# Transposing all of Q by DMA in a fused attention, spectral and feed-forward kernel

## The chip, the cores and the metric

The kernel runs on one core of a Trainium2 chip. The metric is the device time of one execution in microseconds (us), lower is better. Before the change the median of three runs was 299.42 us (298.74 to 299.74). One core has five engines that work side by side, each through its own instruction stream in a fixed order: TensorE (PE; PEld is its weight load), VectorE (DVE), ScalarE (ACT), GpSimd (POOL) and SyncE (SP). Transfers go through sixteen DMA engines. In this kernel GpSimd issues nearly all loads ("software_dynamic" in the profile), and SyncE issues five small ones at the start, the DMA transposes, the stores and some small copies ("hardware_dynamic").

## The reference

Attention with sorted keys and values (4 batches, 8 heads, sequence 768, head width 64), then a two-dimensional Fourier transform over sequence and model width (512), then layer normalisation and a feed-forward part. Cut to what matters:

```python
for _ in range(5):                       # Sinkhorn: P becomes a soft permutation of 8 blocks
    P = P - np.max(P, axis=-1, keepdims=True)
    P = np.exp(P)
    P = P / (np.sum(P, axis=-1, keepdims=True) + 1e-09)
    P = P / (np.sum(P, axis=-2, keepdims=True) + 1e-09)
k_sorted = np.einsum('bhij,bhjcd->bhicd', P, k_b).reshape(B, H, S, D)
v_sorted = np.einsum('bhij,bhjcd->bhicd', P, v_b).reshape(B, H, S, D)
# per block of 96 rows: softmax(q k^T / 8) v
...
X = np.fft.fft(np.fft.fft(x, axis=1), axis=2)
u = x + np.real(X)
un = (u - mu) / np.sqrt(var + 1e-06)
return u + np.maximum(un @ w_ch1, 0.0) @ w_ch2
```

The scores need Q with the head width on the partitions, so Q has to be transposed. So do the normalised rows `un` ahead of the feed-forward matmuls.

## The kernel before

The kernel does not run its statements in the order in which they are written. Each operation is handed to a planner, with what it reads and writes, a priority, and for each engine that may do it a pair of times: how long it holds the engine and when its result is there. The planner simulates the engines once, at build time, and the order that comes out is frozen into the instruction streams. A wrong pair of times gives no wrong result, but an order that fits another machine.

Q of batches 2 and 3 is loaded in small pieces and transposed by DMA. Q of batches 0 and 1 is loaded in long pieces, copied into another order of columns, transposed on TensorE and moved from its bank to SBUF:

```python
QB = (2, 3)
...
many("qr", 2, [128, 6, 128], F16)
many("qt", 3, [128, S], F16)
...
def load_qk(nm, b, hf, prio):
    src = {"k": k, "q": q}[nm]
    if nm == "q" and b in QB:
        for h in range(4):                                  # pieces of 64 elements
            load(kq[:, slot[nm, b, hf], :].rearrange(
                "p (a r h d) -> p a h r d", a=2, h=2, d=D)[:, h // 2, h % 2],
                src[b, 4 * hf + h].rearrange("(r p) d -> p r d", r=6),
                196608, [("kq", slot[nm, b, hf])], prio + 0.01 * h)
        return
    load(kq[:, slot[nm, b, hf], :].rearrange("p (h x) -> p h x", h=4),
         src[b, 4 * hf:4 * hf + 4, :, :].rearrange(
             "h (p r) d -> p h (r d)", r=6), 786432,
         [("kq", slot[nm, b, hf])], prio)
...
def q_copy(b, hp):                                          # batches 0 and 1 only
    if b in QB:
        return
    qr = Buf("qr")
    ...
    P.add(c, lambda e: copy(e, qr.ap.rearrange("p r (h d) -> p r h d", h=2), src), ...)
...
    if b in QB:                                             # in kqt(b, hp)
        qt = Buf("qt")
        P.add({"SP": (1.4, 3.4)}, lambda _: nc.sync.dma_start_transpose(
            qt.ap.rearrange("p (r s) -> p r s", r=6),
            kq[:, slot["q", b, hf], 768 * hl:768 * hl + 768]),
            r=[("kq", slot["q", b, hf])], w=[qt], tag="qX")
        return
    ...
    for r in range(6):
        nc.tensor.matmul(p16[:, 128 * r:128 * r + 128], qr.ap[:, r],
                         idh, is_transpose=True)
    ...
    P.add(c, lambda e: copy(e, qt.ap.rearrange("p (s r) -> p s r", r=6),
          pt.ap.bitcast(F16)[:, 0:768].rearrange("p (r s) -> p s r", r=6)),
          r=[pt], w=[qt], tag="qtev")
```

Note the pair `(1.4, 3.4)`: the planner counts on a transpose landing 3.4 us after SyncE took it up.

The normalised rows of batches 1 to 3 go by DMA as well (`if b > 0:` ahead of `dma_start_transpose(ut..., un)`), those of batch 0 on TensorE. When the planner chooses the next operation of an engine, one of higher priority that lacks a free buffer holds back those of lower priority on the same engine that want a buffer of the same pool.

The softmax here doesn't subtract the row's maximum and nothing guards it: scores larger than these inputs give would overflow.

## Time and profile before

| what | before |
|---|---|
| median of 3 runs | 299.42 us |
| span of the profiled run | 299.0 us |
| first matmul of V's mixing | 30.5 us |
| VectorE busy, 45 to 60 us | 14.84 of 15 us |
| first feed-forward matmul | 76.0 us |
| from there to the end | 223.0 us |
| a transpose of Q (128 x 768) from issue to landing, 98 to 107 us (two of four are recorded) | 2.7 us |

How to read it: the kernel has a stage up to 76 us in which attention and the Fourier part of the first batch are prepared with all engines at work, and a stage after it in which TensorE is full. What moves the border between them moves the end. One caution on this profile: the profiled run took 300.78 us, and later runs of the same kernel lay between 294.3 and 301.9 us (39 in one call, median 297.32). On one core a run counts as slow if it lies over 1.5% above the fastest, so this profiled run and some of the timed ones count as slow; with one core there is no second die to compare with.

### The profile page before, as it was taken

How to read it: one execution, taken by the hardware profiler on the slowest of the kernel's cores; microseconds unless marked ns; L12 is line 12 of the kernel's file. 1: busy time of each engine (PE TensorE's matmuls, PEld its weight loads, DVE VectorE, ACT ScalarE, POOL GpSimd, SP SyncE). 2: the span in 40 equal slices, each digit the busy share in tenths (PEclk: the TensorE clock that was granted, in tenths of full speed). 3: DMA queues.
4: the chain of work that ended last, by engine and by line, in shares of the span. 5: the costliest groups of instructions: out<-in, count | busy, mean ns of one | idle time of the engine just before them, and what ended most of it. 6: DMA issues, size and time to landing. Idle time of an engine off the chain costs nothing.

```text
span 299.0 us, 5829 instructions
## 1 busy us (share of the span) xinstructions
PE 271.8 (91%) x2332; PEld 166.4 (56%) x2332; DVE 178.3 (60%) x395; ACT 153.3 (51%) x307; POOL 55.1 (18%) x91
## 2 busy tenths in 40 slices
PE   0499988884999999899999999999999999999994
PEld 0266976763556656555556645545645645645641
DVE  4797589999699999786249954314605315312001
ACT  2575579862647797468237703613721631641710
POOL 8964212012800036030002000200200010010000
PEclk9999999996699999999999999999999999999999
DMA  7999999980920249825010210031021121121002
GB/s 116 218 286 216 216 206 213 203 111 15 67 17 2 58 98 162 150 13 107 35 71 15 55 70 35 20 105 38 15 53 70 37 53 70 37 54 70 37 0 105
DMA packets 43025, 26.32 MB, mean 88 GB/s; under 512 B 29834, under 2 KB 38552, under 8 KB 42996
## 3 DMA queue, kind: packets, MB, share of 16 engines
q0 software_dynamic: 22576, 15.16, 33.3%
q1 hardware_dynamic: 20422, 10.78, 12.4%
q8 instruction: 18, 0.29, 0.4%
q14 instruction: 9, 0.07, 0.1%
HBM read 28.95 MB, written 6.29 MB: 118 GB/s over the span
## 4 chain that ended last, share of the span: by engine, by line
PE 72%; DVE 16%; DMA 4%; ACT 2%; issue 2%; POOL 2%; DVEq 0%; ACTq 0%; POOLq 0%
PE bank L1112 28%; PE bank L1091 25%; PE bank L635 3%; DVE rt L905 2%; DMA kq<-in_q_dram 2%; PE bank L1005 2%; PE bank L952 2%; PE bank L851 2%; PE bank L891 2%; DMA out_dram<-u 2%; PE bank L638 2%; DVE pmt L919 2%; PE bank L797 2%; DVE u L1020 1%; PE bank L1012 1%
## 5 line engine op out<-in xcount | busy, mean ns | idle before, releaser
L1103 ACT ACTIVATE hr<-bank 128x384 f16<-128x384 f32 x111 | 54.1, 490 | 79.9 <-PE bank L1091 79.7
L1091 PE MATMUL bank<-ut,w1sb 128*128 128x384 f16 x512 | 93.4, 331 | 0.7 <-DVE hr L1100 0.7
L1112 PE MATMUL bank<-w2sb,hr 128*128 128x512 f16 x384 | 89.0, 379 | 0.0
L1091 PEld LDWEIGHTS <-w1sb 128*128 128x128 f16 x512 | 49.5, 99 | 36.1 <-issue 3.0
L1112 PEld LDWEIGHTS <-hr 128*128 128x128 f16 x384 | 36.5, 98 | 40.6 <-issue 0.2
L1120 DVE TENSOR_TENSOR u<-bank,u 128x512 f32<-128x512 f32 x24 | 16.6, 690 | 51.5 <-PE bank L1112 51.0
L1020 DVE SCALAR_TENSOR_TENSOR u<-rt,bank 128x512 f32<-128x512 f16 x24 | 16.1, 678 | 35.6 <-PE bank L1012 29.7
L860 ACT ACTIVATE ex<-bank 96x384 f32<-96x384 f32 x64 | 27.9, 485 | 8.3 <-PE bank L851 6.5
L1033 POOL TENSOR_SCALAR mv<-mv 128x3 f32<-128x3 f32 x8 | 2.6, 320 | 141.8 <-DVE mv L1028 139.6
L1052 ACT ACTIVATE un<-u,nm,ny 128x512 f16<-128x512 f32 x14 | 11.4, 811 | 14.6 <-POOL nm L1042 9.0
L395 POOL DMA_DIRECT2D kq<-in_q_dram x20 | 17.7, 905 | 4.2 <-ACT qr L571 1.9
L891 PE MATMUL bank<-vsf,eb 97*128 97x65 f16 x384 | 15.8, 195 | 2.7 <-DVE u L1020 1.3
L905 DVE TENSOR_TENSOR rt<-bank,rz 128x384 f16<-128x384 f32 x32 | 17.3, 550 | 0.4
L874 ACT ACTIVATE eb<-ex,negone 96x384 f16<-96x384 f32 x29 | 17.5, 614 | 0.2
L891 PEld LDWEIGHTS <-eb 97*128 97x128 f16 x384 | 14.3, 98 | 4.8 <-issue 2.9
L571 ACT CAST vsf<-bank 96x512 f16<-96x512 f32 x19 | 13.9, 790 | 4.3 <-PE bank L638 3.4
L1026 DVE BATCH_NORM_STATS2 st<-u 128x6 f32<-128x512 f32 x24 | 15.9, 682 | 0.2
L395 POOL DMA_DIRECT2D kq<-in_k_dram x8 | 6.5, 808 | 49.9 <-issue 27.8
L826 PE MATMUL bank<-pack,qr 128*128 128x128 f16 x48 | 5.3, 264 | 11.0 <-ACT qr L571 10.2
L635 PE MATMUL bank<-bdv,vcx 128*128 128x128 f16 (+1 forms) x128 | 14.2, 238 | 1.1 <-ACT bdv L571 1.1
L872 DVE TENSOR_SCALAR eb<-ex 96x384 f16<-96x384 f32 x35 | 13.1, 377 | 1.7 <-ACT ex L860 1.6
L797 PE MATMUL bank<-bdk,kq 128*64 128x128 f16 x192 | 11.8, 247 | 1.5 <-DVE u L1020 1.0
(114 smaller groups left out, 337.8 us busy)
## 6 DMA issues: line engine op xcount, KB each, us to landing
out_dram<-u SPq DMA_DIRECT2D x24, 256.0 KB, 2.0
kq<-in_k_dram POOLq DMA_DIRECT2D x8, 384.0 KB, 9.2
w1sb<-in_moe_w_ch_dram POOLq DMA_DIRECT2D x4, 512.0 KB, 15.2
w2sb<-in_moe_w_ch_dram POOLq DMA_DIRECT2D x4, 512.0 KB, 19.0
kq<-in_q_dram POOLq DMA_DIRECT2D x4, 384.0 KB, 11.3
hr<-in_v_dram POOLq DMA_DIRECT2D x2, 768.0 KB, 11.5
kq<-in_v_dram POOLq DMA_DIRECT2D x2, 768.0 KB, 21.3
kq<-in_q_dram POOLq DMA_DIRECT2D x16, 96.0 KB, 6.0
```

The source lines that it names most:

```text
L395: return P.add({eng: c}, lambda _: e.dma_start(dst, src), r=r, w=w, prio=prio, nbytes=nbytes, tag="load", after=after)
L635: nc.tensor.matmul(o, vcx[:, 96 * d:96 * d + m], bd, start=True, stop=(t == 1))
L797: nc.tensor.matmul(ps.ap[64 * h2:64 * h2 + 64, 128 * r3:128 * r3 + 128], k16[:, 2 * hl + h2, 3 * half + r3, :], bdk[:, 2 * hp + h2].rearra ...
L860: nc.scalar.activation(ex.ap, pss[h2].ap[0:96, 0:384], AF.Exp, scale=SCALE),
L874: nc.scalar.activation(ed, src, AF.Identity, bias=negone[0:96])
L891: nc.tensor.matmul(po.ap[:, 65 * T:65 * T + 65], eb.ap[:, e0:e0 + 128], vsf[:, vi:vi + 65], start=(n == 0), stop=(n == 1), skip_group_chec ...
L905: P.add({"DVE": (0.45, 0.56)}, lambda _: V.tensor_tensor(rt.ap[:, :, D * h:D * h + D], po3()[:, :, 0:D], rz.ap[:, :, None].broadcast_to([1 ...
L1020: V.scalar_tensor_tensor(u.ap.rearrange("p (m n) -> p m n", n=2), rt.ap[:, T, :].rearrange("p (m n) -> p m n", n=2), RSC, ps.ap.rearrange( ...
L1091: nc.tensor.matmul(ps.ap[:, 0:GT], w1sb[:, c, 128 * fc:128 * fc + 128], ut.ap[:, c, :], start=(c == 0), stop=(c == 3))
L1103: nc.scalar.activation(hr[g][:, fc, :], ps.ap[:, 0:GT], AF.Relu)
L1112: nc.tensor.matmul(ps.ap, hr[g][:, fc, 128 * tt:128 * tt + 128], w2sb[:, fc, :], start=(fc == 0), stop=(fc == 15))
L1120: V.tensor_tensor(u.ap, ps.ap, u.ap, op=ALU.add),
```

## The change

It is meant to relieve the evacuating engines and TensorE: all of Q goes the way of batches 2 and 3, and the second half of batch 0's normalised rows goes by DMA too. The copies into `qr` fall away, and their space goes to two more `qt` buffers. A key for each head in a slot of `kq` lets a transpose start when its two heads have landed. The claim on a buffer is now ranked over all engines. The 260000 is the size that the planner reckons with for a small load. Cut to its core:

```diff
-QB = (2, 3)
+QB = (0, 1, 2, 3)
...
+            want = {}
+            for e in free:
+                for o in avail[e]:
+                    if o.fresh and o.ready[e] <= free[e] + 0.3:
+                        for p in slot_time(o, ())[1]:
+                            want[p] = min(want.get(p, o.prio), o.prio)
...
-                held = set()
...
-                        st, short = slot_time(o, held)
-                        if o.ready[e] <= t + 0.3:
-                            held |= short
+                        st, short = slot_time(
+                            o, [p for p in want if want[p] < o.prio])
...
-    many("qr", 2, [128, 6, 128], F16)
-    many("qt", 3, [128, S], F16)
+    many("qt", 5, [128, S], F16)
...
+    def kqk(n):
+        return [("kq", n, h) for h in range(4)]
...
-                    196608, [("kq", slot[nm, b, hf])], prio + 0.01 * h)
+                    260000, [("kq", slot[nm, b, hf], h)], prio + 0.01 * h)
...
-                r=[("kq", slot["q", b, hf])], w=[qt], tag="qX")
+                r=kqk(slot["q", b, hf])[2 * hl:2 * hl + 2], w=[qt],
+                tag="qX")
...
-            if b > 0:
+            if b + g > 0:
                 P.add({"SP": (1.3, 3.0)}, lambda _, tt=tt, un=un:
                       nc.sync.dma_start_transpose(
```

Left out here: the other places where the key of a whole slot becomes four keys, and a key for each of the three row copies into `rb`.

More of the change, by code (lines that the diff above doesn't have):

```diff
@@ L422, in load_qk @@
                  "h (p r) d -> p h (r d)", r=6), 786432,
-             [("kq", slot[nm, b, hf])], prio)
+             kqk(slot[nm, b, hf]), prio)
     def hk(g):
@@ L432, in load_v @@
             [("nat", t, hf)] + (hk(0)[8 * hf:8 * hf + 8] if t == 0 else
-                                [("kq", 2 * hf), ("kq", 2 * hf + 1)]), prio)
+                                kqk(2 * hf) + kqk(2 * hf + 1)), prio)
     def load_w1(c, prio):
@@ L581, in v_path @@
         psm = Buf("pm", "pf") if t else Buf("pm")
-        stage = [("kq", n) for n in range(4)] if t else hk(0)
+        stage = [i for n in range(4) for i in kqk(n)] if t else hk(0)
         for hf in range(2):
@@ L755, in a_rows @@
         o = 32 * (b % 2)
-        for dst, src in ((rb[0:32, :], rr[o:o + 32, 0, :]),
-                         (rb[32:64, :], rr[64 + o:96 + o, 0, :]),
-                         (rb[64:96, :], rr[o:o + 32, 1, :])):
+        for n, (dst, src) in enumerate((
+                (rb[0:32, :], rr[o:o + 32, 0, :]),
+                (rb[32:64, :], rr[64 + o:96 + o, 0, :]),
+                (rb[64:96, :], rr[o:o + 32, 1, :]))):
             P.add({"SP": (0.1, 2.3)}, lambda _, dst=dst, src=src:
                   nc.sync.dma_start(dst, src),
-                  r=[("rr", i) for i in (0, 1, 2, 3, 256)], w=["rb"],
+                  r=[("rr", i) for i in (0, 1, 2, 3, 256)], w=[("rb", n)],
                   tag="arow")
@@ L782, in q_copy @@
             e, qr.ap.rearrange("p r (h d) -> p r h d", h=2), src),
-            r=[("kq", slot["q", b, hf])], w=[qr], tag="qcp",
+            r=kqk(slot["q", b, hf])[2 * hl:2 * hl + 2], w=[qr], tag="qcp",
             after=[exps[-1]] if first else [])
@@ L801, in f @@
                             bdk[:, 2 * hp + h2].rearrange("p i c -> p (i c)"))
-            P.add(pe(0.22), f, r=[("kq", slot["k", b, hf]),
+            P.add(pe(0.22), f, r=kqk(slot["k", b, hf]) + [
                                   ("bdk", hp // 2)],
@@ L1016, in dft2 @@
                   r=[y4[c][g] for c in range(4)]
-                  + ["rb", "rrow", "lt", "lt96", "lt96a", "lt96b", "dtab"],
+                  + [("rb", n) for n in range(3)] + ["rrow", "lt", "lt96", "lt96a", "lt96b", "dtab"],
                   w=[ps, u], tag="dft2")
```

## The prediction

> **What bounds the kernel now.** I read the page first, slice by slice, because the average (TensorE busy 91%) mixes stages.
>
> ```profile
> PE   0499988884999999899999999999999999999994
> DVE  4797589999699999786249954314605315312001
> ACT  2575579862647797468237703613721631641710
> ...
> PEclk9999999996699999999999999999999999999999
> DMA  7999999980920249825010210031021121121002
> ```
>
> A slice is 7.5 us. From slice 11 on TensorE is full: the feed-forward matmuls (lines 1091 and 1112) alone are 53% of the chain that ended last. Its idle time is before that: 299.0 - 271.8 = 27.2 us, of which some 10 at the start, 4 in the tail, and most of the rest between 40 and 76 us. The feed-forward part starts at 76 us; whatever moves that start moves the end nearly one for one. So I asked next what fills 40 to 76 us, with busy times by stretch (columns: stretch, length, then PE, PEld, DVE, ACT, POOL busy with their counts, granted clock, DMA share, GB/s):
>
> ```profile
> 45.00:50.00 5.00, 4.29 (x94) 3.42 (x95) 4.97 (x17) 4.65 (x12) 0.79 (x2) 1.00 1.24 207
> 50.00:55.00 5.00, 4.38 (x68) 3.88 (x68) 4.94 (x13) 4.21 (x11) 0.80 (x1) 1.00 1.12 222
> 55.00:60.00 5.00, 3.83 (x63) 3.10 (x60) 4.94 (x13) 4.95 (x10) 0.00 (x0) 1.00 1.22 196
> 60.00:65.00 5.00, 4.71 (x72) 3.68 (x73) 4.99 (x15) 4.89 (x12) 0.76 (x1) 1.00 0.77 91
> 65.00:70.00 5.00, 3.13 (x31) 2.06 (x29) 5.00 (x12) 0.00 (x0) 0.00 (x0) 1.00 0.47 70
> ```
>
> VectorE is full from 45 to 72 us, ScalarE nearly so until 65: this stage is bound by the two evacuating engines, not by TensorE. The chain of waits of the same stage shows the instructions that the change removes, and the end of the stage, where it removes nothing:
>
> ```profile
> 45.09 0.86 DVE qt L571
> ...
> 46.68 0.27 DVE qr L571
> ...
> 70.33 0.90 POOL ny L1036
> ...
> 71.87 0.82 ACT un L1052
> 72.69 0.05 issue
> 72.74 0.62 PE bank L1071 x4
> 73.39 0.05 issue
> 73.43 0.82 ACT un L1052
> ```
>
> Lastly GpSimd's own order in time, since it issues all loads:
>
> ```profile
> 18.87 0.74 POOL L395 DMA_DIRECT2D kq<-in_k_dram  x1 [1.23 <-DMA kq<-in_k_dram]
> 20.90 1.28 POOL L395 DMA_DIRECT2D kq<-in_q_dram  x1 [1.29 <-DMA kq<-in_q_dram]
> ```
>
> These are loads 13 and 14; they wait for a K and a Q load, and counting back these are loads 5 and 6 (all later waits up to load 22 fit the same distance). I read this as at most eight loads in flight: load n waits for load n-8.
>
> **What the Trainium skill says.** "DMA: Bandwidth & Descriptors", Specifications, wants at least 512 B per piece for line rate. The new Q layout lands in pieces of 64 f16 = 128 B, where the old one has 768 B. The trace agrees in direction: six such loads of batch 2 were issued from 75.8 to 81.5 us, 5.71 / 6 = 0.95 us each, with the DMA engines full behind them, so about 3.8 us for half a batch; the old form's half (384 KB) took about 1.9 us, the step from 18.9 to 20.9 us above. The same page, Queues, rings and completion order, says that an engine takes turns between the queue rows; a transpose from SyncE must therefore share with the loads. Here the small row copies of SyncE took 4.9 us to land in the busy stretch 40 to 62 us and 1.8 us in a quiet one. "TensorE: Matmul & The Clock Gate", Part 1, has the array at half clock until it has been busy for some 3.4 us, and again after an idle window. The trace agrees: the 128-column matmuls of lines 635 and 638 follow each other at 0.107 us until 36 us and 0.056 us afterwards, and the first twelve of line 1091, after the thin stretch 67 to 75 us, take 3.95 us where twelve later take 1.95.
>
> **The change, part by part.**
>
> Removed on TensorE: 48 Q transposes and 12 of the 24 for the normalised rows. In a warm stream that is 60 x 0.056 = 3.4 us, but the 48 lie before 60 us, where TensorE isn't the bound. The 12 come at 79.8 to 82 us, inside the half-clock stretch: 12 x 0.107 = 1.3 us of TensorE's full time, so about 1 us on the path.
>
> Removed on ScalarE and VectorE: eight copies into qr and eight evacuations into qt. ScalarE has five of each (828 and 803 ns: 8.2 us), VectorE three of each (347 and 950 ns: 3.9 us). By place: at 9 to 12 us one pair each delays the Sinkhorn chain, whose reduction waits until 11.96 us though the exponential was ready to start at 9.83; 1.6 us come free there. At 26 to 30 us four more. In 40 to 52 us VectorE loses 0.25 + 0.86 + 0.27 = 1.4 us of its full time. In 54 to 60 us ScalarE loses four, some 0.75 us apart, 3.0 us, while the first DFT's evacuations wait behind them (TensorE's dft1 stood 0.94 us for the qt evacuation, which held a bank). Balanced over the two engines and allowing for the chain's VectorE work, which stays, I take 2 us of those 3. Sum for 40 to 76 us: 3.4 us.
>
> Added: 8 + 3 transposes on SyncE, 1.2 us of issue each, 2.7 us to land when quiet, perhaps 5 to 6 here. SyncE is otherwise idle, and only two head pairs of batch 0 can be scored before V is mixed (four eb buffers, two a pair), so these latencies are mostly hidden. DMA: 4 x (3.8 - 1.9) = 7.6 us for the loads. The four transposes at 98 to 107 us sum to 4.0 us of DMA share in the stretches there, 1 us each: 8 us more. The full stretch, now until 62 us, ends near 76. What lands last in it (w2, then V of batches 2 and 3, wanted at 83 us) has 20 us or more of slack, so this costs little.
>
> Moved, and this is where I hesitate: before the memsets GpSimd now has 14 loads in place of 8. By the depth of eight the 14th waits for the sixth, V's first half, which lands at 13.0 now and, behind Q's extra 1.9 us and a transpose, at 15 to 16. The memsets ran from 6.64 to 14.1 us, 7.5 us long; they would then run from about 16.5 to 24. The first write into eb (21.3 us now) needs all of them, so it slips by some 2.7 us. Against it stand the 1.6 us of Sinkhorn, the four removed instructions at 26 to 30 us and 2.2 us of VectorE idle at 20 to 30 us. I call it even: V's mixing starts at 30.5 +- 1.5 as now.
>
> The ranking of buffer claims over all engines matters for the qt pool, which SyncE's prefetches and TensorE's a_path now share; I count it as what keeps the gain, with none of its own.
>
> Sum: 0 before 40 us, 3.4 in 40 to 76, 1 after: 4.4 us, so 299.4 - 4.4 = 295 us.
>
> **Rivals.** (a) The memset block costs more than the slack there: the in-order queues of ScalarE and VectorE stall at the first eb write with V's copies behind it. The waits of loads 13 to 22 speak for it; VectorE's idle 2.2 us speaks against the full size. It would give 298 to 301. (b) The freed evacuators bring the start forward by all they lost in 40 to 60 us (4.4 us), the Sinkhorn's 1.6 us come through too, and a shorter gap at 67 to 75 us spares the cold clock (2 us): 290 to 292. Against it: the chain from u over GpSimd's power to the transposed rows, 66 to 76 us, is untouched for the first half. (c) Everything is hidden, because the DFT chain of batch 0 is latency and other attention work of batch 1 fills what is freed: 298 to 299, the 1 us alone.
>
> **Range and chances.** The centre is 295; (a) and (b) lie some 5 us to either side and I hold them about equally likely, with a new static order as a further 2 us of noise. So 289.5 to 300.5 for 8 in 10. Faster by over 2% means below 293.4: 0.33. Slower by over 2%, above 305.4, needs the memset block and a bad order together: 0.05.
>
> **What would show it.** Right: the first feed-forward matmul at 72 to 73 us; no qr, and no qt evacuations of 128x768; GpSimd's memsets ending near 24 us with waits on Q loads before them; V's mixing starting near 30; the DMA row full to about 76 us; from there a TensorE stage as long as before, less 1 us. Wrong: V's mixing starting after 32 us (then a), the feed-forward starting before 70 us (then b), TensorE idle in 85 to 125 us on a load, or a transpose as the releaser of scores for more than 1 us in total.

## The result and the profile after

The changed kernel is correct and slower: a median of 312.28 us (311.19 to 314.79, four runs, all fast) against 299.08 us of before on the same chip (294.53 to 299.74, four runs, of which two count as fast). The ratio is 1.054, with a 95% interval of 1.037 to 1.071. Here and below a ratio is the mean time of one kernel's fast runs over that of the other's of the same rounds, so it is not quite the ratio of the medians quoted beside it.

The page first. These are the same five rows as in the prediction, now of the changed kernel (busy tenths in 40 slices of 7.7 us, granted clock, DMA share):

```profile
PE   0367991589499999879999999999999999999995
...
DVE  4778882569967999879514986414532422421002
ACT  2446762563445892559604751641661442452610
...
PEclk9977897559769999999999999999999999999999
DMA  9999999999918001995010111021121012012002
```

Slices 7 to 9 of PE, which start at 46, 54 and 62 us, read 1, 5 and 8, where the old kernel had 8, and the granted clock below them falls to half. DVE, which was to be relieved, isn't full there any more: it reads 2, 5, 6. The DMA row is full to about 84 us instead of 62. The windows between 45 and 70 us say it more sharply (columns as in the prediction: stretch, length, busy PE, PEld, DVE, ACT, POOL, clock, DMA share, GB/s):

```profile
45.00:50.00 5.00, 2.34 (x52) 1.74 (x50) 3.56 (x13) 3.47 (x9) 1.26 (x2) 1.00 1.08 210
50.00:55.00 5.00, 0.00 (x0) 0.00 (x0) 0.00 (x0) 0.00 (x0) 0.00 (x0) 0.52 1.15 189
55.00:60.00 5.00, 3.15 (x52) 2.53 (x52) 2.98 (x8) 3.35 (x7) 1.65 (x2) 0.50 1.23 196
60.00:65.00 5.00, 3.35 (x52) 2.67 (x52) 3.42 (x6) 3.22 (x8) 1.64 (x2) 0.50 1.24 203
65.00:70.00 5.00, 4.33 (x43) 3.59 (x44) 3.63 (x9) 2.36 (x6) 1.57 (x2) 0.50 1.06 217
```

For five whole microseconds no engine does anything, while the DMA engines are full. Then comes a stretch of at least 15 us at half clock. Who held them up is in the chain that ended last, in order of time (start, length, what it waited on):

```profile
8.60 11.87 DMA qt<-kq
20.52 0.50 PE bank L859 x8
...
42.93 17.54 DMA qt<-kq
60.47 0.05 issue
60.52 0.55 PE bank L859 x8
```

Two transposes of Q stand on it with 11.87 and 17.54 us, from SyncE's issue to landing (for the second, whose landing isn't recorded, to the scores that waited for it). The first belongs to batch 0, the second to batch 1. On the whole page these transposes make 10% of the chain, 29 us, and TensorE's scores stood 12.6 us for them:

```profile
L859 PE MATMUL bank<-qt,ks 64*128 64x96 f16 x256 | 13.6, 226 | 18.2 <-DMA qt<-kq 12.6
```

The timeline of TensorE shows why a late transpose of batch 1 stopped batch 0 (start, length, instruction, in brackets the idle time before it and its releaser):

```profile
55.63 0.50 PE L859 MATMUL bank<-qt,ks 64*128 64x96 f16 x8 [7.88 <-DMA qt<-kq]
56.06 1.50 PE L899 MATMUL bank<-vsf,eb 97*128 97x65 f16 x24
57.50 0.50 PE L859 MATMUL bank<-qt,ks 64*128 64x96 f16 x8
57.93 0.85 PE L804 MATMUL bank<-bdk,kq 128*64 128x128 f16 x12
60.52 0.82 PE L859 MATMUL bank<-qt,ks 64*128 64x96 f16 x16 [1.74 <-DMA qt<-kq]
```

The scores at 55.63 are batch 1's first; their transpose was issued at 41.54 us and landed 14.0 us later. Right behind them, with no wait, come 24 matmuls of attention times V for batch 0. Their operands must have been done before 50 us, since no engine worked from 50 to 55. They stood behind the scores only because TensorE's order is fixed, and the planner, which reckoned with 3.4 us, had put batch 1's scores first. All that hangs on batch 0 (its Fourier part, its normalised rows, the feed-forward start) stood with them.

How long the eight transposes for batches 0 and 1 took to land, from the view of the tile `qt` between 5 and 80 us (six of the eight have a recorded landing), and the DMA queues between 50 and 62 us (packets, MB, share; q0 carries GpSimd's loads, q1 SyncE's transposes and row copies):

```profile
DMA to landing us min/median/max: 4.4/12.2/19.4
```

```profile
q0 software_dynamic: 1726, 1.89, 91.2%
q1 hardware_dynamic: 1729, 0.43, 28.1%
```

While the loads were under way the two queues got through the same number of packets, but a load's packet carried 1.89 MB / 1726 = 1.1 KB and one of the other queue 0.43 MB / 1729 = 250 B. So SyncE's queue, the transposes and the small row copies together, got 0.43 MB / 12 us = 36 GB/s, and 196 KB at that rate take 5.4 us each, one behind the other. Alone in its queue row at 98 to 107 us of the old profile, the same instruction ran at some 215 GB/s.

These turns are not all of it. The transposes issued at 8.60 and at 41.54 us found none before them in their queue, and yet the trace has no packet of theirs for the first 3.9 and 3.7 us. In the quiet stretch of the old kernel the first packet came 1.2 to 1.3 us after the issue (98.32 and 103.24 us). What holds the first packet back is not settled; e12_bench below shows it too.

The lateness also fed back on the loads. Batch 2's Q goes into the slots that batch 1's transposes read, so GpSimd, which issues those loads, stood 15.5 us for transposes (the page):

```profile
L398 POOL DMA_DIRECT2D kq<-in_q_dram x32 | 27.1, 873 | 25.7 <-DMA qt<-kq 15.5
```

How much of the loss this makes is not shown.

The border of the stages is the first matmul of line 1091 before, of line 1099 after; first a line of before, then one of after:

```profile
75.99 4.02 PE L1091 MATMUL bank<-ut,w1sb 128*128 128x384 f16 x12
```

```profile
85.91 1.44 PE L1099 MATMUL bank<-ut,w1sb 128*128 128x384 f16 x4 [0.68 <-DVE ut L577]
```

It moved by 9.9 us. From it to the end the old kernel took 299.0 - 76.0 = 223.0 us, the new one 309.3 - 85.9 = 223.4 us. So of the 10.3 us between the two profiles practically all are lost before the border. Because before's profile is of a slower run, I also took the fast profiled run of an almost equal kernel (e2_ux below, 296.07 us): there the border is at 73.1 us of 294.3, and 12.8 of the 15.0 us to the new span are lost before it.

Two things happened as predicted. The memsets on GpSimd were pushed back behind the small loads and ended at 18.11 + 4.00 = 22.1 us; the load ahead of them waited for V's first half (GpSimd's timeline):

```profile
13.60 0.67 POOL L398 DMA_DIRECT2D vcx<-k_lt  x1 [2.38 <-DMA hr<-in_v_dram]
...
18.11 4.00 POOL L451 MEMSET eb<- 96x1536 f16 x3
```

And V's mixing began at 30.54 us in both kernels. Against the 28.30 us of the fast profile of e2_ux that is 2.2 us later, so this agreement owes something to the slow profile of before.

### The profile page after: what moved, and what is told of

Its sections match the earlier page's. It is cut to its first block, busy times and chain, and to the rows that moved or that the text cites.

```text
span 309.3 us, 5743 instructions
## 1 busy us (share of the span) xinstructions
PE 267.5 (86%) x2272; PEld 163.2 (53%) x2272; DVE 175.2 (57%) x386; ACT 146.9 (47%) x297; POOL 66.4 (21%) x103
## 4 chain that ended last, share of the span: by engine, by line
PE 75%; DMA 13%; DVE 7%; issue 1%; POOL 1%; ACT 1%; DVEq 0%; SPq 0%; POOLq 0%
PE bank L1099 27%; PE bank L1120 27%; DMA qt<-kq 10%; PE bank L960 4%; PE bank L641 3%; PE bank L899 3%; PE bank L1013 2%; PE bank L859 2%; DMA out_dram<-u 2%; DMA kq<-in_q_dram 2%; PE bank L592 2%; PE bank L804 2%; PE bank L644 1%; DVE u L1028 1%; PE bank L1020 1%
## 5 line engine op out<-in xcount | busy, mean ns | idle before, releaser
L1099 PE MATMUL bank<-ut,w1sb 128*128 128x384 f16 x512 | 94.7, 331 | 0.7 <-DVE ut L577 0.7
L398 POOL DMA_DIRECT2D kq<-in_q_dram x32 | 27.1, 873 | 25.7 <-DMA qt<-kq 15.5
L859 PE MATMUL bank<-qt,ks 64*128 64x96 f16 x256 | 13.6, 226 | 18.2 <-DMA qt<-kq 12.6
L859 PEld LDWEIGHTS <-ks 64*128 64x128 f16 x256 | 8.3, 103 | 24.4 <-DMA qt<-kq 11.7
L882 ACT ACTIVATE eb<-ex,negone 96x384 f16<-96x384 f32 x35 | 20.8, 609 | 0.2
L899 PE MATMUL bank<-vsf,eb 97*128 97x65 f16 x384 | 18.2, 206 | 2.3 <-DVE rt L913 1.5
L899 PEld LDWEIGHTS <-eb 97*128 97x128 f16 x384 | 16.5, 106 | 5.3 <-issue 3.5
L577 ACT CAST vsf<-bank 96x512 f16<-96x512 f32 x17 | 12.7, 794 | 7.0 <-PE bank L641 4.3
L641 PE MATMUL bank<-bdv,vcx 128*128 128x128 f16 (+1 forms) x128 | 12.8, 228 | 0.1
L880 DVE TENSOR_SCALAR eb<-ex 96x384 f16<-96x384 f32 x29 | 10.3, 359 | 3.3 <-ACT ex L868 3.3
```

The costliest lines, as they stand in the source:

```text
L398: return P.add({eng: c}, lambda _: e.dma_start(dst, src), r=r, w=w, prio=prio, nbytes=nbytes, tag="load", after=after)
L641: nc.tensor.matmul(o, vcx[:, 96 * d:96 * d + m], bd, start=True, stop=(t == 1))
L859: nc.tensor.matmul(pss[h2].ap[:, BLK * j:BLK * j + BLK], ks.ap[rows, 4 * g + j, :], qt.ap[rows, c0:c0 + BLK])
L882: nc.scalar.activation(ed, src, AF.Identity, bias=negone[0:96])
L899: nc.tensor.matmul(po.ap[:, 65 * T:65 * T + 65], eb.ap[:, e0:e0 + 128], vsf[:, vi:vi + 65], start=(n == 0), stop=(n == 1), skip_group_chec ...
L1099: nc.tensor.matmul(ps.ap[:, 0:GT], w1sb[:, c, 128 * fc:128 * fc + 128], ut.ap[:, c, :], start=(c == 0), stop=(c == 3))
```

## The experiments

My theory after the result: the transposes are late because they share the DMA engines with full load queues, and TensorE's fixed order turns the lateness into a standstill. The rivals: the small pieces of the loads cost the time (A); the ranking of the claims made a bad order (B); the transposes of the normalised rows did (C). All twelve kernels gave the right result. Each has beside it the median of before: 296.58 us (7 runs) for the first four, 297.69 us (7 runs) for the next four, 297.32 us (39 runs) for the last four.

| run | what it is | median us | ratio to before (95%) | first feed-forward matmul |
|---|---|---|---|---|
| e9_xno | after, Q of batches 0 and 1 on TensorE | 298.99 | 1.008 (1.002 to 1.013) | 77.8 |
| e3_small | before, small loads with one key per slot | 319.18 | 1.072 (1.065 to 1.079) | not used |
| e10_unrank | after, old claim rule | 311.74 | 1.051 (1.045 to 1.058) | 88.9 |
| e2_ux | before, with the three normalised-row transposes | 297.18 | 0.999 (0.991 to 1.007) | 73.1 |
| e4_lat | after, planner told 16 us | 316.69 | 1.066 (1.057 to 1.075) | 89.8 |
| e8_hold | after, W2 and V held back | 324.79 | 1.091 (1.081 to 1.102) | 83.3 |
| e6_x0 | batch 0 alone by DMA | 305.12 | 1.026 (1.018 to 1.035) | 79.3 |
| e7_x1 | batch 1 alone by DMA | 315.67 | 1.054 (1.042 to 1.065) | 96.1 (a slow run) |
| e12_bench | before, with a measuring tail | 334.75, one look | none | none |
| e3b_small | before, small loads with a key per head | 302.86 | 1.022 (1.015 to 1.030) | 78.7 |
| e5_d64 | before, Q transposed without the copy | 293.61 | 0.992 (0.989 to 0.995) | 72.0 |
| c1_d64_ux | e5_d64 and e2_ux together | 293.69 | 0.991 (0.988 to 0.995) | not used |

**e9_xno: take the transposes away, keep the rest.** The small pieces happen to lie so that TensorE can transpose them without a copy, so this run undoes only the DMA transposes for batches 0 and 1. The move from the bank into `qt` is then a plain copy (0.56 us on VectorE, against 0.95 in before, where it reorders).

```diff
-        if b in QB:            # QB = (0, 1, 2, 3)
+        if b in QX:            # QX = (2, 3): transpose by DMA
...
-                nc.tensor.matmul(p16[:, 128 * r:128 * r + 128], qr.ap[:, r],
-                                 idh, is_transpose=True)
+                o = 768 * hl + 128 * r
+                nc.tensor.matmul(p16[:, 128 * r:128 * r + 128],
+                    kq[:, slot["q", b, hf], o:o + 128],
+                    idh, is_transpose=True)
...
```

> The changed kernel with its Q loads in small pieces and its ranking, but Q of batches 0 and 1 transposed on TensorE again, straight from the loaded pieces (no copy into qr, 8 evacuations into qt remain). Theory A, that the loss is the SyncE transposes landing 12 to 19 us after issue in the full DMA stretch and TensorE standing in order behind them (12.6 us of waits before the scores): without them the feed-forward starts near 75 us instead of 86, and the time is 296 to 301 us. Rival B, that the small-piece loads delay V, K and the memsets and cost the time whatever transposes: V's mixing and the feed-forward start stay late and the time stays at 308 to 314.

It came to 298.99 us (298.3 to 299.39), ratio 1.008. The kernel that has the transposes is at 1.054, so about 4.6% or 13.8 us hang on this one part (13.0 us against e10_unrank, 1.051). The standstill at 50 us is gone (the same columns as above):

```profile
50.00:55.00 5.00, 3.96 (x78) 3.04 (x75) 5.00 (x14) 4.43 (x10) 1.27 (x3) 1.00 1.24 207
```

What is left is a loss of 0.8%, although eight copies fewer should have gained.

**e3_small: the small loads alone.** Before, with all Q loaded in small pieces and still copied and transposed on TensorE.

```diff
-        if nm == "q" and b in QB:
+        if nm == "q":
```

> The kernel before with one thing changed: Q of batches 0 and 1 is loaded in the small pieces (32 loads of 96 KB in place of 4 of 384 KB and 16 of 96 KB), still copied into qr and transposed on TensorE. It measures the small loads alone, with the memsets behind 14 loads. Theory A: within 2 us of the kernel before (297 to 302), with the memsets ending near 22 us. Rival B: 306 or more.

It came to 319.18 us, which no theory had. The profile shows that the edit was flawed: with one key for the whole slot the planner takes the four loads of a slot for four writers in a row and spreads them out, and TensorE stood 18.8 us for a copy of Q (its timeline, of a slow run; the four fast runs took 316.93 to 321.31 us):

```profile
54.01 1.46 PE L826 MATMUL bank<-pack,qr 128*128 128x128 f16 x12 [18.78 <-DVE qr L571]
```

So this run says nothing on the DMA cost of small pieces. It does show what the key for each head in the change is for. It was repeated with such keys as e3b_small.

**e10_unrank: the change with the old claim rule.** The diff is the ranking above, the other way round.

> The changed kernel with the old rule for buffer claims (each engine ranks its own). Theory A: the transposes land as late as in the changed kernel, so 308 to 316 us. Rival C, that the new ranking made a bad static order: 295 to 302. If the ranking was what kept the order sound, it would be worse than 316.

311.74 us, ratio 1.051: the loss is there without the ranking. B falls. In this other order TensorE's scores stood 14.5 us for transposes, so the wait doesn't hang on one order. (The reverse, the ranking on the old kernel alone, could not be built: the planner found no operation that it could place. So whether the ranking helps anything stays open.)

**e2_ux: the three normalised-row transposes alone.**

```diff
-            if b > 0:
+            if b + g > 0:
```

> The kernel before with only the normalised rows of batch 0's second half transposed by DMA. By the prediction's sum about 1 us faster (12 TensorE transposes at half clock and three evacuations go); theory A gives 297 to 300 us, since these transposes come after the full DMA stretch. If these transposes had a share in the loss, slower than 302.

297.18 us, ratio 0.999 with an interval of 0.991 to 1.007. C falls as a loss, and the 1 us that I had predicted as a gain wasn't seen either.

**e4_lat: tell the planner the truth.** If the standstill comes only from a plan that counts on 3.4 us, a plan that counts on 16 should heal it.

```diff
-            P.add({"SP": (1.4, 3.4)}, lambda _: nc.sync.dma_start_transpose(
+            P.add({"SP": (1.4, 16.0 if b < 2 else 3.4)}, lambda _: nc.sync.dma_start_transpose(
```

> The changed kernel with the planner told that a Q transpose of batches 0 and 1 takes 16 us to land in place of 3.4; the same instructions, in another static order. If the loss is the in-order wait of TensorE for scores that were placed as though the transposes took 3.4 us, most of it comes back: waits of the scores for the transposes under 4 us (12.6 now), 298 to 304 us. If the loss is the lateness itself, whatever the order, it stays at 308 to 315.

This missed: 316.69 us (316.1 to 330.23, the last a slow run). The scores' wait for transposes did fall, from 12.6 to 3.5 us, but other waits took its place (the view of waits: who waited for whom, us in total, times, longest):

```profile
ACT un L1060 <- POOL nm L1050: 15.0, 2, 14.5
...
PE bank L1079 <- ACT ex L868: 13.8, 1, 13.8
...
POOL kq L398 <- DMA w2sb<-in_moe_w_ch_dram: 10.3, 4, 4.0
```

GpSimd stood in its own order with loads that waited for W2's loads and, last of all, 5.0 us for a transpose; behind them stood the small operations that the normalisation of batch 0 needs, and ScalarE waited for these 14.5 us in one piece. The order changed, but the lateness stayed: between 5 and 60 us the transposes took 9.8 to 22.3 us to land.

**e8_hold: take the big loads away from the transposes.** W2 and the second loads of V wait until batch 1's last transpose of Q has landed; the wait is a small copy on GpSimd that reads its result. The old claim rule is used, since e10_unrank had cleared it.

```diff
+            if b == 1 and hp == 3:
+                holds.append(P.add({"POOL": (0.2, 0.3)}, lambda _: nc.gpsimd.tensor_copy(
+                    tick, qt.ap[0:1, 0:1]), w=["tick"], prio=-300.0,
+                    after=[P.ops[-1]], tag="tick"))
...
-             1048576, [("w2", c)], prio)
+             1048576, [("w2", c)], prio, after=holds)
```

> The changed kernel (with the old claim rule, which measured the same: 311.7) and one more tiny GpSimd copy that reads the last Q transpose of batch 1; GpSimd issues W2's and V's second loads only after it. It empties the DMA queue beside the transposes of batch 1. Theory A, contention: batch 1's transposes land in 3 to 7 us (14 to 19 in the changed kernel), the feed-forward starts at 72 to 78 us and the time is 294 to 302. If the lateness came from the transposes waiting for buffers or for Q and not from the full queue, no change: 308 to 315.

The transfer part came out in part, the time did not. Two of batch 1's four transposes have a recorded landing: the one issued at 43.72 us, while the loads of W1 were under way, took 11.6 us, and the one issued at 56.59, where the queue was now emptier, 3.6.

But the time rose to 324.79 us, outside both expected ranges. GpSimd stood 14.6 us, from 41.9 to 56.5; the view of waits names no cause, the view of the tile `qt` puts it down to a transpose of Q. So Q's next loads were late as well. The loads held back went out from 63 us on. The next three transposes of Q, issued at 61.49, 63.52 and 76.65 us, took 9.7, 14.6 and 19.0 us, and VectorE waited 14.0 us in one piece for one of the normalised rows (view of waits):

```profile
DVE un L1065 <- DMA ut<-un: 17.9, 2, 14.0
```

So lateness follows the large loads: moving the loads moved it. As a repair this version is no good, and as a test of the total it is not clean.

**e6_x0 and e7_x1: one batch each.** As e9_xno with `QX = (0, 2, 3)` and `QX = (1, 2, 3)`, both with the old claim rule.

> As the kernel with small loads and TensorE transposes (299.0 us), with the old claim rule, but batch 0's Q transposed by DMA and only batch 1's on TensorE. Its transposes landed in 12, 12, 4 and 7 us and the first two held the scores up for 3 us. Expected 299 to 304 us, against 299 with none by DMA: a small part of the loss.

> The mirror: batch 0's Q on TensorE, batch 1's by DMA. These are the transposes that landed 14 to 19 us after issue beside W1, W2 and V and held scores up for 7.9 and 1.7 us, with the clock falling to half afterwards. Expected 306 to 313 us: nearly the whole loss.

Batch 0 alone gave 305.12 us (1.026), a little above the expected range, with 1.9 us of scores' wait and 4.4, 11.0 and 12.4 us as least, median and most to land between 5 and 60 us. Batch 1 alone gave 315.67 us (1.054), above the expected range too and as much as the whole change. Its profiled run counted as slow; the scores' wait in it is the largest of all runs, though from a slow run only its kind is taken (view of waits):

```profile
PE bank L856 <- DMA qt<-kq: 19.3, 3, 9.8
```

So batch 1's transposes, which have W1, W2 and V beside them and batch 0's work behind them, are the costly ones. Over e9_xno the two halves lose 1.8% and 4.6%, and the whole 4.6%, so they don't add up. That a standstill which two waits share is paid once would explain it, but it is not shown.

**e12_bench: the disputed figure by itself.** Behind the old kernel's last work, three transposes of Q each time: alone, beside four loads of W2, and beside small-piece loads of Q.

```diff
+        three()                                   # alone
...
+        for c in range(4):
+            G.dma_start(w2sb[:, 4 * c:4 * c + 4, :], w2v[:, 4 * c:4 * c + 4, :])
...
+        three()                                   # beside W2
...
+        for h in range(8):
+            G.dma_start(kq[:, 4 + h // 4, :]...[:, (h % 4) // 2, h % 2],
+                q[3, h].rearrange("(r p) d -> p r d", r=6))
...
+        three()                                   # beside small pieces
```

> The kernel before with a measuring tail after its last result: three Q transposes of 192 KB alone, three beside four W2 loads (2 KB rows in the source), three beside small-piece Q loads. Only the times from issue to landing count, not the total. Theory A, a transpose takes turns with the loads packet by packet: alone 2.7 to 4 us to land; beside W2 12 to 20 us; beside the small pieces clearly less than beside W2, 4 to 8 us, because a turn of the loads is then short. If the lateness in the changed kernel came from something else (buffers, Q's own loads), all three groups land in under 6 us.

The DMA view of the three stretches, in this order (the last number is the median us to landing; all three landings are recorded in the middle group, one in each of the others):

```profile
qt<-kq SPq DMA_TRANSPOSE x3, 2.8
```

```profile
qt<-kq SPq DMA_TRANSPOSE x3, 10.6
```

```profile
qt<-kq SPq DMA_TRANSPOSE x3, 6.0
```

The order is as expected, and the middle figure is a little under its range. Beside W2 the lateness has two parts. The first transpose was issued at 303.91 us, and up to 308.3 only the loads moved packets; from 308.3 to 316 both queues did, in similar numbers (the DMA view of the windows 303.9:308.3 and 308.3:316, in this order):

```profile
q0 software_dynamic: 736, 0.74, 111.7%
```

```profile
q0 software_dynamic: 1184, 1.17, 89.4%
q1 hardware_dynamic: 1413, 0.35, 32.9%
```

In the second stretch the transposes got some 45 GB/s. Beside the small pieces (3491 packets of the loads for 0.44 MB, some 125 B each, 323.4 to 331 us) the first packet came 1.5 us after the issue, and the transposes got through their 0.59 MB in 7.6 us, some 78 GB/s. So in these runs the transposes got more bytes beside small packets, and the wait for the first packet is a part of its own, which turns by packets don't explain.

**e3b_small: the small loads alone, with keys.** Before, with the loads and keys of the change, the old rule, copies and TensorE transposes kept.

```diff
-        if b in QB:            # transposes, QB = (0, 1, 2, 3) for the loads
+        if b in QX:            # QX = (2, 3); qr and the copies stay
```

> The small loads alone again, now with one key for each head as the changed kernel has it (the first attempt kept one key for four loads, which chained them in the plan and spread them over 50 us). Copies, TensorE transposes and the old claim rule as in the kernel before. Theory A: 298 to 302 us. Rival B: 306 or more.

302.86 us (301.53 to 303.61), ratio 1.022, just above the range of theory A. The memsets ended at 22.3 us, as in the changed kernel, and the first feed-forward matmul was at 78.7 us. V's mixing began at 29.3 us, 1.0 us after e2_ux. So A has a share: 2.2% or 6.6 us, as far as this run is the loads alone (in the new layout the plain copies on VectorE took 0.56 us into `qr` and 0.54 into `qt`, against 0.34 and 0.95 before). Through which wait they cost that isn't settled; TensorE's wait for Q's copies grew only from 10.9 to 12.0 us.

**e5_d64 and c1_d64_ux: a better way to drop the copies.** Before, with the long loads unchanged, but Q of batches 0 and 1 transposed on TensorE head by head, straight from the loaded slot. That makes 96 transposes of 64 columns out of 48 of 128, and no copy; `qt` has five buffers, as in the change.

```diff
-            for r in range(6):
-                nc.tensor.matmul(p16[:, 128 * r:128 * r + 128], qr.ap[:, r],
-                                 idh, is_transpose=True)
+            for r in range(6):
+                for h2 in range(2):
+                    nc.tensor.matmul(
+                        p16[64 * h2:64 * h2 + 64, 128 * r:128 * r + 128],
+                        qk16("q", b, hf)[:, 2 * hl + h2, r, :],
+                        idh, is_transpose=True)
```

> A try at a better kernel: the kernel before, loads unchanged, but Q of batches 0 and 1 transposed on TensorE straight from where it was loaded, head by head (96 transposes of 64 columns in place of 48 of 128), so that the eight copies into qr go; five qt buffers. It takes 4.1 us from ScalarE and 1.0 from VectorE and adds some 2.7 us to TensorE at a place where TensorE isn't the bound. Expected 1 to 3 us faster than the kernel before: 294 to 297.

> The same, and the normalised rows of batch 0's second half by DMA. By itself that part measured -0.1% (+-0.8). Expected 293 to 297 us, 1% under the kernel before at best.

e5_d64 came to 293.61 us (expected 294 to 297; 22 runs, 291.81 to 296.49), ratio 0.992, interval 0.989 to 0.995. It beats both kernels, if only by 0.8% over before. The normalised-row transposes add nothing to it: 293.69 us (18 runs), 0.991.

## Why the prediction was wrong

Predicted were 295.0 us, and at most 300.5; measured were 312.28.

**The step that failed** is this one: "2.7 us to land when quiet, perhaps 5 to 6 here", and from it "these latencies are mostly hidden". Both halves failed. The transposes took 4.4 to 19.4 us, a median of 12.2 over the six that are recorded. The size had been taken from the row copies into `rb` in the busy stretch, 4.9 us, but these are of 32 KB. A transpose has 196 KB in packets of some 250 B, and beside loads it gets about one packet for each of theirs: 1729 against 1726. Where its queue was empty before it, it moved no packet at all for the first 3.7 to 4.4 us beside large loads, against 1.2 to 1.3 us in a quiet stretch. Alone it lands in 2.8 us, beside W2 in a median of 10.6, in one and the same program (e12_bench). And the latency wasn't hidden, because hiding needs other work that the engine may do. I had argued from the buffers (two head pairs of batch 0 may be scored early), and overlooked batch 1: the planner had put its scores ahead of batch 0's attention times V. Undoing this part alone brings back 13.8 us (e9_xno), and batch 1's transposes alone cost as much as the whole change (e7_x1).

**A second term was mis-sized.** "7.6 us" more DMA time for the loads was to cost "little". The 3.8 and 1.9 us behind it were spacings between issues on GpSimd, not transfer times. With copies and TensorE transposes kept, the small loads cost 2.2%, 6.6 us (e3b_small). The four ratios form a ladder: before 1.000; with small loads 1.022; with the copies dropped too 1.008 (e9_xno, which also has the ranking, the normalised rows and five `qt` buffers); with the transposes by DMA 1.054. In microseconds of a 297 us kernel that is +6.6, -4.3, +13.8. The steps come from different calls, and the middle one lumps several edits, so it is a rough account.

**The gain never had a place to show.** The 3.4 us for 40 to 76 us rested on VectorE and ScalarE being the bound there. They were no longer: with the scores late VectorE was busy 6.55 of 15 us between 45 and 60, against 14.84 before. That the removed copies are worth something is shown where the loads and the DMA transposes stay as they were: e5_d64, 0.8% or 2.5 us, though it keeps the evacuations.

**One reading was loose.** The prediction has the clock rise after some 3.4 us of work and says that the trace agrees. In its own lines TensorE ran without a break from 30.54 us on, and the spacing fell only at 36 us, 5.5 us later. Nothing in the sum rests on it.

**The 1 us after the border** was not seen: 223.4 us against 223.0 in the profiles (221.2 in e2_ux's), and e2_ux at 0.999 with an interval that would hold a gain of 0.3% as well.

**What was right.** The depth of eight loads, with V's first half as what the last load ahead of the memsets waits for; the memsets' end (24 predicted, 22.1 measured); the 1.6 us of the Sinkhorn chain (VectorE's last instruction of it ended at 11.72 us instead of 13.38); and that the ranking adds nothing of its own to this result (e10_unrank, 1.051 against 1.054). V's mixing "as now" (30.54 in both) was partly luck: against the fast profile of e2_ux it is 2.2 us late. The DMA row was full to about 84 us, not 76. The rivals were all about memsets and freed engines, and none was the cause; but the list of what would show the prediction wrong had "a transpose as the releaser of scores for more than 1 us in total", and that was 12.6 us. I had the right observation to look for and gave it almost no weight: 0.05 for slower.

**What stays open.** How much of the 13.8 us is the standstill itself and how much the half clock that follows it, from 50 to at least 70 us, could not be separated, since no run kept one without the other. e4_lat and e8_hold removed most or part of the scores' wait, but opened others of 14 us, so no run shows the transposes of batches 0 and 1 by DMA with a good order. That the DMA engines take turns by packets is read from the counts, and what holds a transpose's first packet back for some 4 us beside large loads is not known.

## What to carry to other kernels

A transfer that is off the busy engines is free only if the queue it joins is quiet when it runs: ask which loads are under way at that time, how large their packets are beside its own, and how many transfers stand ahead of it in its own row. And where the order of an engine is fixed at build time, a latency that is planned at 3.4 us and takes 12 costs not only its own consumer but everything that stands behind that consumer. Before removing a copy by a transfer, try to remove it where it is: here a transpose that reads the loaded layout directly gained 0.8%, while the transfers lost 5.4%.

## What the Trainium skill lacked or had wrong

- "Advanced Engine Details and Errata", X-Bar Transpose (TRN2), says that transpose DMAs are as fast as regular ones, and expects 350 to 400 GB/s. Here a 128 x 768 transpose ran at some 215 GB/s alone (2.7 to 2.8 us to land), and beside loads at 36 to 45 GB/s (10.6 us to land beside W2, up to 19.4 us in the kernel). The page doesn't say what becomes of a transpose beside other traffic.
- "DMA: Bandwidth & Descriptors", Queues, rings and completion order, has each engine take turns between queue rows packet by packet. The counts agree, if a packet of the profile is one of the page's (1726 and 1729 in 12 us; 1184 and 1413 beside W2 from 308.3 us on). What it lacks is the consequence: the row with 250 B packets gets under a fifth of the bytes (0.43 of 2.32 MB) beside one with 1.1 KB packets. It also lacks the time to the first packet of a transpose beside large loads: 3.7 to 4.4 us here, 1.2 to 1.3 in a quiet stretch.
- "VectorE: DVE Perf Modes", The three transpose paths, gives one time for a 128 x 128 transpose through the crossbar, 1309 ns, against 390 ns on TensorE. Six of them in one instruction took 2.8 us here when alone, and 4.4 to 19.4 us when not; a single figure misleads for the choice between the paths, though its advice to use TensorE where the bank can be the destination agrees with e5_d64 and e9_xno.
- No page that I consulted names the depth that bounded GpSimd's loads here: load n waited for load n-8. Ahead of the memsets this wait was 2.4 us; their end went from 14.1 to 22.1 us, the rest of it because six more loads are issued before them.
